# Two attention blocks in one TensorE stream: V copies placed three items ahead, output projections spread over the loop, a cast-free tail and a reordered start

## The chip, the cores and the metric

The kernel runs on one core of one Trainium2 chip; the other cores are idle. The metric is the device time of one execution in microseconds (us). Most executions of one kernel agree within 0.3%. Each experiment was timed in rounds that alternate with the kernel before on the same chip.

## The reference

Two cached attention blocks, their outputs side by side. A has 8 key/value heads, each shared by 4 of the 32 query heads; B has 32 heads of each kind. Batch 8, 64 query tokens, model width 512, 2048 cached keys, head size 128, everything in bf16.

```python
def block(x, k_cache, v_cache, wq, wo):          # A: k, v repeated 4 times along the heads
    q = (x @ wq).reshape(B, Sq, 32, 128).transpose(0, 2, 1, 3)
    p = softmax(einsum("bhqd,bhkd->bhqk", q, k) * 128 ** -0.5)
    o = einsum("bhqk,bhkd->bhqd", p, v)
    return o.transpose(0, 2, 1, 3).reshape(B, Sq, 4096) @ wo
return concatenate([block_A, block_B], axis=-1)   # 8 x 64 x 1024
```

The caches are 335 MB, each byte is used once, and the kernel transposes every K tile on the chip. On the page of the kernel before TensorE is busy 96% of the span, and the packets of the load queue take 90.7% of the span of the DMA engines.

## The kernel before

Python builds one list of operations for each engine, with hand-written semaphore waits; the order in the lists is the order on the engines. The attention work is 1024 *items*: even items are a quarter of an A half-unit (four 128-key tiles, two query heads), odd items half of a B unit (eight key tiles, one head). Sixteen items hold one A unit (one K/V head of one batch entry) and four B units. In the code `G` stands for A and `M` for B. An *evacuation* is the copy of a group's results out of PSUM, the memory that the matmuls write to.

```python
    for t in range(NI):                          # NI = 1024
        for key in chunks_at.get(t, []):
            do_chunk(key)                        # 8 key transposes (TensorE), evacuation (VectorE)
        for n in vcopies_at.get(t, []):
            do_vcopy(n)                          # V into a tile with a column of ones (VectorE)
        for use in proj_at.get(t, []):
            do_proj(use)                         # QM, QG: queries of B, A; WA, WB: output of A, B
        if t + 2 < NI:
            do_qk(t + 2)                         # scores (TensorE), exp (ScalarE)
        for gk in ot_pending.pop(t, []):
            do_ot(gk)                            # transpose of a finished output, copy (VectorE)
        do_pv(t)                                 # value product; at a group's end reciprocal, normalization
```

Where a V copy stands: five items before the first use, on VectorE, for both kinds of units. The copy also decides when the next V is requested, since the staging buffer has four slots:

```python
    def vcopy_place(n):
        f = first_item(*units[n])
        pl = f - (VLEAD_POOL if vcopy_eng(n) == "pool" else VLEAD_DVE)    # VLEAD_DVE = 5
    ...
    for it in sorted(k for k in vcopies_at if k < 0):    # before the loop: in order of slots
        for n in vcopies_at[it]:
            do_vcopy(n)
    ...
        if n >= NVT:                                     # NVT = 4, the V load of unit n
            vneeds.append(vcopy_val[n - NVT])
    reqs.sort(key=lambda r: (r[0], r[1], r[2]))          # r[0]: when the last need is produced
```

Output projections: four heads at a time, four token tiles (`tt`) of 128 rows, i.e. two batch entries each. All of them wait for the last batch entry, then come four items apart, and write the one shared PSUM bank `MISC`, which the query projections and the output transposes use too; an add on VectorE accumulates them in f32.

```python
    for s in range(NSA):
        lastL = last_item("G", s * Bn + Bn - 1)
        for tt in range(NTT):
            it = lastL + 8 + 4 * tt              # for B: lastL + 10 + 4 * tt
            if it < NI: sched(it, ("WA", s, tt))
            else: epi.setdefault(tt, []).append(("WA", s, tt))
    ...
            dvv = DV.add(lambda e, ...: e.tensor_tensor(
                outacc[:, tt, cols], region, outacc[:, tt, cols], ALU.add), ...)
            bank_reader[bank] = (dve_W, dvv)     # the bank's next writer waits for this add
```

The tail casts the sums to bf16 (two tiles on VectorE, two on ScalarE) and stores them from SyncE and ScalarE.

The softmax here doesn't subtract the row's maximum and nothing guards it: scores larger than these inputs give would overflow.

Of the kernel before, what the change touches and what calls it, by code (L numbers as in the profile page):

```python
# [4 lines left out]
ACTF = mybir.ActivationFunctionType  # L5
# [60 lines left out]
def bass_concat_heads__gqa_block_cached__mha_block_cached__near_ridge_kernel(  # L66
# [122 lines left out]
    dve_W = sem("dve_W")  # L189
    dve_F = sem("dve_F")  # L190
    pool_I = sem("pool_I")
# [77 lines left out]
    prologue_proj = []  # L269
    for h in range(HM):  # L270
        use = ("QM", h)
        if h == 0:
            prologue_proj.append(use)
        else:
            lo = 0 if h < 2 else last_item("M", (h - 2) * Bn + Bn - 1) - 1
            sched(max(lo, first_item("M", h * Bn) - 17), use)
    for hk in range(HG):
        for i in range(4):
            use = ("QG", hk, i)
            if hk == 0:  # L280
                prologue_proj.append(use)
            else:
                lo = 0 if hk < 2 else last_item("G", (hk - 2) * Bn + Bn - 1) - 1
                sched(max(lo, first_item("G", hk * Bn) - 44 + 8 * i), use)
    NSA = HG
    NSB = HM // 4
    epi = {}
    for s in range(NSA):
        lastL = last_item("G", s * Bn + Bn - 1)
        for tt in range(NTT):  # L290
            use = ("WA", s, tt)
            it = lastL + 8 + 4 * tt
            if it < NI:
                sched(it, use)
            else:
                epi.setdefault(tt, []).append(use)
    for s in range(NSB):
        lastL = last_item("M", (4 * s + 3) * Bn + Bn - 1)
        for tt in range(NTT):
            use = ("WB", s, tt)  # L300
            it = lastL + 10 + 4 * tt
            if it < NI:
                sched(it, use)
            else:
                epi.setdefault(tt, []).append(use)
# [11 lines left out]
    def V_src(kind, u):  # L317
        if kind == "G":
# [5 lines left out]
    out_v = out.rearrange("b q e -> (b q) e").rearrange("(tt p) e -> p tt e", p=P)  # L324

    PO.add(lambda e: e.memset(ident[:], 0.0), inc=pool_I)
    PO.add(lambda e: e.affine_select(out=ident[:], in_=ident[:], compare_op=ALU.not_equal,
                                     fill=1.0, base=0, pattern=[[-1, P]], channel_multiplier=1),
           needs=[(pool_I, 1)], inc=pool_I)
    for i in range(NVA):  # L330
        PO.add((lambda i: lambda e: e.memset(vaug[:, i, :, P:VW], 1.0))(i), inc=pool_I)
    PO.add(lambda e: e.memset(outacc[:], 0.0), inc=pool_I)
    PO.add(lambda e: e.memset(scr[:], 0.0), inc=pool_I)
    PO.add(lambda e: e.memset(pT[:], 0.0), inc=pool_I)
    PO.add(lambda e: e.memset(onM[:], 0.0), inc=pool_I)
    POOL_INIT_DONE = PO.count[pool_I]
    IDENT_READY = 2

    AC.add(lambda e: e.activation(scr[:, 1:2], scr[:, 0:1], ACTF.Exp), needs=[(pool_I, POOL_INIT_DONE)])
    xT_ready = {}  # L340
# [13 lines left out]
    woev_val = {}  # L354
    lastadd = {}

    for n in range(NU):
# [8 lines left out]
    def vcopy_place(n):  # L366
        f = first_item(*units[n])
        pl = f - (VLEAD_POOL if vcopy_eng(n) == "pool" else VLEAD_DVE)
        if n >= NVA:
            pl = max(pl, last_item(*units[n - NVA]) + 1)  # L370
        assert pl <= f, (n, pl, f)
        return pl
# [5 lines left out]
    def do_vcopy(n):  # L378
        needs = [(semV[n % NVT], 16 * (n // NVT + 1)), (pool_I, POOL_INIT_DONE)]
        if n >= NVA:  # L380
            occ = units[n - NVA]
            needs.append((pe_PV, pv_val[last_item(*occ)]))
        va = n % NVA
        vt = n % NVT
        if vcopy_eng(n) == "dve":
            v = DV.add(lambda e: e.tensor_copy(  # L386
                vaug[:, va, :, 0:P], vtmp[:, vt, :].rearrange("p (kt d) -> p kt d", d=P)),
                needs=needs, inc=dve_V)
            vcopy_val[n] = (dve_V, v)
        else:  # L390
            srcv = vtmp[:, vt, :].bitcast(dt.int32).rearrange("p (kt d) -> p kt d", d=P // 2)
            dstv = vaug[:, va, :, :].rearrange("p kt c -> p (kt c)").bitcast(dt.int32).rearrange(
                "p (kt c) -> p kt c", c=VW // 2)[:, :, 0:P // 2]
            v = PO.add(lambda e: e.tensor_copy(dstv, srcv), needs=needs, inc=pool_V)
            vcopy_val[n] = (pool_V, v)
# [31 lines left out]
    def do_proj(use, bank=MISC):  # L427
# [46 lines left out]
        else:  # L474
# [4 lines left out]
            ob = ob_A if prob == "A" else ob_B  # L479
            wo = wo_A if prob == "A" else wo_B  # L480
            needs.append((semWo[sl], 16 * (s // 2 + 1)))
            if prob == "A":
                lastg = ("G", s * Bn + Bn - 1, 1)
            else:
                lastg = ("M", (4 * s + 3) * Bn + Bn - 1, 0)
            needs.append((dve_C, copy_val[lastg]))

# [11 lines left out]
            if key in lastadd:  # L499
                dneeds.append((dve_W, lastadd[key]))  # L500
            dvv = DV.add(lambda e, tt=tt, cols=cols, region=region: e.tensor_tensor(  # L501
                outacc[:, tt, cols], region, outacc[:, tt, cols], ALU.add), needs=dneeds, inc=dve_W)
            lastadd[key] = dvv
# [3 lines left out]
    def do_qk(t):  # L507
# [38 lines left out]
        qk_val[t] = v  # L546
        aneeds = [(pe_S, v), (pool_I, POOL_INIT_DONE)]
        slot = t % NPT
# [10 lines left out]
    def do_pv(t):  # L559
# [31 lines left out]
        if glast:  # L591
# [12 lines left out]
            else:  # L604
# [9 lines left out]
                bank_reader[OMB] = (act_N, nv)  # L614
            norm_val[gkey] = nv

    OT_DELAY = 4

    def do_ot(gkey, bank=None):
        kind, u, pr = gkey  # L620
        bank = MISC if bank is None else bank
        needs = [(act_N, norm_val[gkey]), (pool_I, POOL_INIT_DONE)] + br(bank)
        mb = bank_bf(bank)
# [37 lines left out]
    def do_xT(prob):  # L661
# [18 lines left out]
        xT_ready[prob] = (dve_X, dv)  # L680

    do_xT("B")
    do_xT("A")

    pro_banks = [MISC, SB[0], SB[1], SB[2], OGB, OMB]
    pchunks = [k for k in chunks if chunk_slot[k] < 0]
# [36 lines left out]
    for idx, use in enumerate(epilogue_proj):  # L723
        do_proj(use, bank=epi_banks[idx % len(epi_banks)])
    act_F = sem("act_F")
    cast_val = {}
    for tt in range(NTT):
        fneeds = [(dve_W, lastadd[(tt, pr_)]) for pr_ in ("A", "B") if (tt, pr_) in lastadd]
        if tt % 2 == 0:
            v = DV.add((lambda tt: lambda e: e.tensor_copy(outbf[:, tt, :], outacc[:, tt, :]))(tt), needs=fneeds, inc=dve_F)  # L730
            cast_val[tt] = (dve_F, v)
        else:
            v = AC.add((lambda tt: lambda e: e.activation(outbf[:, tt, :], outacc[:, tt, :], ACTF.Copy))(tt),
                       needs=fneeds, inc=act_F)
            cast_val[tt] = (act_F, v)

# [28 lines left out]
    for h in range(HM):  # L765
        needs = []
        desired = first_item("M", h * Bn) - 17 - LEADW
        if h >= 2:
            needs.append((pe_W, proj_val[("QM", h - 2)]))
            needs += lead_need(desired)  # L770
        else:
            desired = -1000 + h
        src = B_wq[:, h * P:(h + 1) * P].rearrange("(ct c) d -> c ct d", c=P)
        reqs.append((SPp.need_pos(needs), desired, -1, needs,
                     (lambda sl, src: lambda e: e.dma_start(wq_M[:, sl, :, :], src))(h % 2, src), semWqM[h % 2]))
    for hk in range(HG):
        needs = []
        desired = first_item("G", hk * Bn) - 44 - LEADW
        if hk >= 2:
            needs.append((pe_W, proj_val[("QG", hk - 2, 3)]))  # L780
            needs += lead_need(desired)
        else:
            desired = -998 + hk
        src = A_wq[:, hk * 4 * P:(hk + 1) * 4 * P].rearrange("(ct c) e -> c ct e", c=P)
        reqs.append((SPp.need_pos(needs), desired, -1, needs,
                     (lambda sl, src: lambda e: e.dma_start(wq_G[:, sl, :, :], src))(hk % 2, src), semWqG[hk % 2]))
    for s in range(NSA):
        needs = []
        desired = last_item("G", s * Bn + Bn - 1) + 8 - LEADW
        if s >= 2:  # L790
# [6 lines left out]
    for s in range(NSB):  # L797
        needs = []
        desired = last_item("M", (4 * s + 3) * Bn + Bn - 1) + 10 - LEADW
        if s >= 2:  # L800
            needs.append((pe_W, proj_val[("WB", s - 2, NTT - 1)]))
        if s >= 1:
# [5 lines left out]

    SPp.add(lambda e: e.dma_start(xn_B[:, :, :], B_x.rearrange("b q c -> (b q) c").rearrange("(tt p) c -> p tt c", p=P)),
            inc=semXB, inc_by=16)  # L810
    SPp.add(lambda e: e.dma_start(xn_A[:, :, :], A_x.rearrange("b q c -> (b q) c").rearrange("(tt p) c -> p tt c", p=P)),
            inc=semXA, inc_by=16)
    for npos, desired, order, needs, fn, s_ in reqs:
        SPp.add(fn, needs=needs, inc=s_, inc_by=16)
    for tt in range(NTT):
        prog = SPp if tt % 2 == 0 else AC
        prog.add((lambda tt: lambda e: e.dma_start(out_v[:, tt, :], outbf[:, tt, :]))(tt),
                 needs=[cast_val[tt]], inc=semOut, inc_by=16)
    SPp.add(lambda e: e.wait_ge(semOut, 16 * NTT) and None, needs=[])
    AC.add(lambda e: e.wait_ge(semOut, 16 * NTT) and None, needs=[])  # L820

# [53 lines left out]
```

## Time and profile before

| | before |
|---|---|
| median of 12 runs | 1074.86 us (1073.12 to 1076.93) |
| profiled span | 1074.5 us |
| first weight load of the value product of item 0 / 16 / 1023 | 22.81 / 38.84 / 1060.24 us |
| from the last of these to the end of the span | 14.24 us |
| bytes moved | 357.13 MB, 332 GB/s over the span |

The third row divides the span into a start (to item 16), a loop and a tail. These starts are read from the timeline of weight loads. In the views, PE stands for TensorE's matmuls, PEld for its weight loads, DVE for VectorE, ACT for ScalarE, POOL for GpSimd and SP for SyncE. A line of a timeline has start and duration in us, engine, line of the kernel, operation, output<-input and shapes; in brackets, how long the engine had been idle and what released it. One more view belongs to the lines that the prediction shows: the waits of TensorE, added up by the line that waited and the line that released it (us in total, times, longest).

```profile
PE ps L631 <- DVE h L501: 7.9, 14, 0.6
PE ps L461 <- DVE h L656: 7.1, 14, 0.5
```

The first is an output transpose that waits for an output add, twice in each of seven periods; the second a query projection of A that waits for the copy of an output transpose. Both are waits for a reader of the one shared bank.

### The profile page before, as it was taken

To read this page: it belongs to the slowest core of one execution; us is meant where nothing else is said; L and a number is where in the kernel's file an instruction comes from. 1 tells how busy PE (TensorE), PEld (TensorE's weight loads), DVE (VectorE), ACT (ScalarE), POOL (GpSimd) and SP (SyncE) were. 2 spreads that over 40 slices of the span, in tenths; PEclk is the share of its full clock that TensorE was granted. 3 is DMA by queue.
4 is the path that set the end of the run, shared out by engine and by line. 5 is a ranking of instruction groups with operands and counts; after the bars stand their busy time and mean duration, and the time that the engine had idled before them with its cause. 6 is when DMAs were issued, how large, how long until landed. Compare 5 with 4: busy or idle time off the path is not lost.

```text
span 1074.5 us, 41588 instructions
## 1 busy us (share of the span) xinstructions
PE 1027.9 (96%) x18247; PEld 957.3 (89%) x18336; DVE 767.6 (71%) x1802; ACT 742.5 (69%) x1476; POOL 8.3 (1%) x17
## 2 busy tenths in 40 slices
PE   6999999999999999999999999999999999999997
PEld 4999888999889998899979999799997999979995
DVE  4777676776777767777767776677676776767775
ACT  3777766777667775677757777577775777757775
POOL 3000000000000000000000000000000000000000
PEclk9999999999999999999999999999999999999999
DMA  9999997999889998799998999899997999979991
GB/s 345 403 375 359 330 317 261 385 361 359 315 278 380 362 353 315 275 381 366 347 311 291 383 364 336 289 332 369 372 327 276 346 350 369 342 256 347 349 359 58
DMA packets 123540, 357.13 MB, mean 332 GB/s; under 512 B 27616, under 2 KB 40928, under 8 KB 123360
## 3 DMA queue, kind: packets, MB, share of 16 engines
q1 hardware_dynamic: 123072, 353.94, 90.7%
q8 instruction: 146, 2.39, 0.9%
q10 hardware_dynamic: 288, 0.52, 0.1%
q14 instruction: 34, 0.28, 0.1%
HBM read 353.37 MB, written 1.05 MB: 330 GB/s over the span
## 4 chain that ended last, share of the span: by engine, by line
PE 82%; DVE 11%; issue 2%; ACT 2%; DMA 2%; SPq 1%; DVEq 0%
PE ps L413 24%; PE ps L586 19%; PE ps L578 10%; PE ps L527 9%; PE ps L542 8%; PE ps L491 5%; DVE h L421 4%; DVE h L386 4%; PE ps L440 2%; PE ps L461 2%; DVE h L501 2%; ACT h L611 1%; PE ps L649 1%; DMA h<-in_B_v_cache_dram 1%; PE ps L631 1%
## 5 line engine op out<-in xcount | busy, mean ns | idle before, releaser
L421 DVE COPY h<-ps 128x1024 bf16<-128x1024 bf16 x640 | 440.2, 688 | 152.1 <-PE ps L413 142.6
L413 PE MATMUL ps<-h 128*128 128x128 bf16 x5120 | 390.3, 219 | 5.8 <-DMA h<-in_B_k_cache_dram 2.4
L555 ACT ACTIVATE h<-ps 128x512 bf16<-128x512 f32 x512 | 305.0, 596 | 103.3 <-PE ps L542 98.5
L550 ACT ACTIVATE h<-ps 128x512 bf16<-128x512 f32 x512 | 305.4, 597 | 91.5 <-PE ps L527 66.8
L586 PE MATMUL ps<-h 128*128 128x129 bf16 x4096 | 323.4, 220 | 6.4 <-issue 0.4
L413 PEld LDWEIGHTS ps<-h 128*128 128x128 bf16 x5120 | 314.3, 98 | 8.6 <-issue 7.1
L586 PEld LDWEIGHTS ps<-h 128*128 128x128 bf16 x4096 | 252.1, 98 | 10.6 <-issue 10.4
L386 DVE COPY h<-h 128x2048 bf16<-128x2048 bf16 x320 | 218.0, 682 | 1.2 <-DMA h<-in_B_v_cache_dram 1.2
L578 PE MATMUL ps<-h 128*128 128x129 bf16 x2048 | 203.4, 221 | 0.0
L542 PE MATMUL ps<-h 128*128 128x64 bf16 x4096 | 202.9, 193 | 0.5 <-issue 0.5
L527 PE MATMUL ps<-h 128*128 128x128 bf16 x2048 | 197.6, 219 | 0.7 <-ACT h L469 0.7
L542 PEld LDWEIGHTS ps<-h 128*128 128x128 bf16 x4096 | 169.4, 98 | 7.4 <-issue 0.8
L527 PEld LDWEIGHTS ps<-h 128*128 128x128 bf16 x2048 | 139.7, 98 | 21.7 <-ACT h L469 1.2
L578 PEld LDWEIGHTS ps<-h 128*128 128x128 bf16 x2048 | 138.6, 98 | 0.0
L611 ACT ACTIVATE h<-ps,h 64x128 bf16<-64x128 f32 x256 | 92.8, 363 | 65.3 <-DVE h L609 42.0
L600 DVE RECIPROCAL h<-ps 128x1 f32<-128x1 f32 x128 | 21.4, 167 | 74.5 <-PE ps L578 74.5
L501 DVE TENSOR_TENSOR h<-ps,h 128x512 f32<-128x512 f32 x64 | 44.1, 689 | 34.3 <-PE ps L491 34.1
L491 PE MATMUL ps<-h 128*128 128x512 bf16 x227 | 58.5, 380 | 5.0 <-ACT h L448 1.6
L649 PE MATMUL ps<-h 128*128 128x128 bf16 x256 | 56.3, 220 | 0.4 <-ACT h L611 0.4
L638 DVE COPY h<-ps 128x128 bf16<-128x128 bf16 x128 | 28.2, 220 | 33.7 <-PE ps L631 28.8
L601 ACT ACTIVATE h<-ps,h 128x128 bf16<-128x128 f32 x128 | 47.3, 369 | 0.3 <-DVE h L600 0.3
L656 DVE COPY h<-ps 128x64 bf16<-128x64 bf16 x256 | 46.4, 181 | 0.7 <-PE ps L649 0.7
(29 smaller groups left out, 266.1 us busy)
## 6 DMA issues: line engine op xcount, KB each, us to landing
h<-in_B_k_cache_dram SPq DMA_DIRECT2D x256, 512.0 KB, 6.5
h<-in_B_v_cache_dram SPq DMA_DIRECT2D x256, 512.0 KB, 6.1
h<-in_A_k_cache_dram SPq DMA_DIRECT2D x64, 512.0 KB, 5.4
h<-in_A_v_cache_dram SPq DMA_DIRECT2D x64, 512.0 KB, 7.4
h<-in_B_wq_dram SPq DMA_DIRECT2D x32, 128.0 KB, 6.8
h<-in_A_wq_dram SPq DMA_DIRECT2D x8, 512.0 KB, 7.7
h<-in_A_wo_dram SPq DMA_DIRECT2D x8, 512.0 KB, 6.2
h<-in_B_wo_dram SPq DMA_DIRECT2D x8, 512.0 KB, 7.8
```

Source lines behind the costliest of these rows:

```text
L386: v = DV.add(lambda e: e.tensor_copy(vaug[:, va, :, 0:P], vtmp[:, vt, :].rearrange("p (kt d) -> p kt d", d=P)), needs=needs, inc=dve_V)
L413: ins = e.matmul(dst[:, j * P:(j + 1) * P], lhsT=kin[:, ks, kt * P:(kt + 1) * P], rhs=ident[:, :], is_transpose=True, start=True, stop=True)
L421: dv = DV.add(lambda e, kb=kb, par=par, c=c, kTX=kTX: e.tensor_copy(kTX[:, par, 8 * c:8 * c + 8, :], bank_bf(kb)[:, 0:8 * P].rearrange("p ...
L491: ins = e.matmul(region, lhsT=ob[:, sl, hh, tt * P:(tt + 1) * P], rhs=wo[:, sl, hh, :], start=(hh == 0), stop=(hh == 3))
L527: ins = e.matmul(ps[:, sbk, j * P:(j + 1) * P], lhsT=kT_G[:, par, kt, :], rhs=rhs, start=True, stop=True)
L542: ins = e.matmul(ps[:, sbk, j * SQ:(j + 1) * SQ], lhsT=kT_M[:, par, kt, :], rhs=rhs, start=True, stop=True)
L550: av = AC.add(lambda e: e.activation(pT[:, slot, 0:512], ps[:, sbk, :], ACTF.Exp, scale=scale), needs=aneeds, inc=act_E)
L555: av = AC.add(lambda e: e.activation(dstv, srcv, ACTF.Exp, scale=scale), needs=aneeds, inc=act_E)
L578: ins = e.matmul(ps[:, OGB, 0:P + 1], lhsT=pT[:, slot, j * P:(j + 1) * P], rhs=vaug[:, va, kt, 0:P + 1], start=(kt == 0), stop=(kt == NKT ...
L586: ins = e.matmul(ps[:, OMB, 0:P + 1], lhsT=pT[:, slot, j * P:(j + 1) * P], rhs=vaug[:, va, kt, 0:P + 1], start=(kt == 0), stop=(kt == NKT ...
L611: nv = AC.add(lambda e: e.activation(onM[0:SQ, par, :], ps[0:SQ, OMB, 0:P], ACTF.Copy, scale=rsM[0:SQ, par:par + 1]), needs=[(dve_R, rv)] ...
L649: return e.matmul(mb[:, 0:P], lhsT=onM[:, par, :], rhs=ident[:, :], is_transpose=True, start=True, stop=True)
```

## The change

The intent is to remove waits from TensorE: (1) A's V copy two items later; (2) each output projection as soon as its own two batch entries are done, so that they are spread and never near another use of the shared bank; (3) a tail with three projections left instead of eight, sums written as bf16 by the last add, stores from GpSimd; (4) x and query weights of A first, finer waits for the initial fills. Core of the diff:

```diff
-        pl = f - (VLEAD_POOL if vcopy_eng(n) == "pool" else VLEAD_DVE)
+        pl = f - (3 if units[n][0] == "G" else VLEAD_DVE)
...
+    def wo_dep_unit(prob, s, tt):
+        b = BPT * tt + BPT - 1
+        return ("G", s * Bn + b, 1) if prob == "A" else ("M", (4 * s + 3) * Bn + b, 0)   # (shortened)
...
-            it = lastL + 8 + 4 * tt
+            it = last_item(gk[0], gk[1]) + 10        # WA; gk = wo_dep_unit("A", s, tt)
-            it = lastL + 10 + 4 * tt
+            it = last_item(gk[0], gk[1]) + 14        # WB
...
-            needs.append((dve_C, copy_val[lastg]))
+            needs.append((dve_C, copy_val[wo_dep_unit(prob, s, tt)]))
...
+            if s == nsess - 1:
+                dvv = DV.add(lambda e, ...: e.tensor_tensor(
+                    outbf[:, tt, cols], region, outacc[:, tt, cols], ALU.add), ...)
+                final_val[key] = dvv
...
-    (four casts of outacc to outbf, on VectorE and ScalarE; four stores, from SyncE and ScalarE)
+        PO.add((lambda tt: lambda e: e.dma_start(out_v[:, tt, :], outbf[:, tt, :]))(tt),
+               needs=[(dve_W, final_val[(tt, "A")]), (dve_W, final_val[(tt, "B")])], inc=semOut, inc_by=16)
...
-    do_xT("B")
     do_xT("A")
+    do_xT("B")
     (request order xA, wqG0, xB, wqM0 ...; exp table loaded after one small fill instead of all)
```

One side effect is not visible in the diff. The copies before the loop are emitted in order of their slots. With A's at -3 and B's still at -4, the first B copy now precedes the first A copy. The V load of the second A unit (needed at item 16) therefore enters the queue before that of the fourth B unit (needed at item 13).

## The prediction

> **What bounds the kernel now.** First the page: the span, the busy shares and the chain of work that ended last.
>
> ```profile
> span 1074.5 us, 41588 instructions
> PE 1027.9 (96%) x18247; PEld 957.3 (89%) x18336; DVE 767.6 (71%) x1802; ACT 742.5 (69%) x1476; POOL 8.3 (1%) x17
> ...
> PE 82%; DVE 11%; issue 2%; ACT 2%; DMA 2%; SPq 1%; DVEq 0%
> ```
>
> TensorE is the bound, but the weight-load row (PEld), which has a record of every load, is busy 957 of 1074 us: up to 117 us in which no new matmul started, some of it the slow tail of 512-column matmuls, the rest waits. The work is a sequence of 1024 items, alternately a quarter of an A half-unit and half of a B unit. 16 items (one A unit, four B units) are one unit of the loop; eight units are one period, after which the extras recur: 4 projections each of kinds QM and QG (queries) and WA and WB (output), 16 in all. So I cut the stretch from 540.5 to 671.7 us, one period, into its eight units, of which five are shown (the cuts are at the first weight load of each unit's first value product); columns are time, busy TensorE, loads, VectorE, ScalarE, GpSimd, clock, DMA share and GB/s.
>
> ```profile
> 540.52:560.80 20.28, 19.39 (x302) 16.42 (x303) 15.29 (x34) 11.51 (x23) 0.00 (x0) 1.00 0.91 318
> 560.80:579.16 18.36, 17.28 (x293) 15.30 (x292) 12.46 (x30) 11.57 (x23) 0.00 (x0) 1.00 0.72 230
> 579.16:594.40 15.24, 15.05 (x285) 14.54 (x284) 12.12 (x29) 11.28 (x23) 0.00 (x0) 1.00 1.01 384
> 594.40:608.77 14.37, 14.23 (x282) 14.13 (x280) 10.39 (x27) 11.26 (x23) 0.00 (x0) 1.00 0.98 373
> ...
> 657.37:671.74 14.37, 14.23 (x281) 14.13 (x279) 10.38 (x27) 11.25 (x23) 0.00 (x0) 1.00 0.94 320
> ```
>
> A unit with no projection takes 14.37 us; one QM adds 0.87 us. All eight output projections sit in the first two units, 20.28 and 18.36 us, where DMA idles; in the rest DMA is nearly full. 16 projections at 0.867 us are 13.9 us, eight bare units 115.0; the period is 131.2, so 2.35 us of it is collision. One looks like this:
>
> ```profile
> 551.55 0.69 DVE L501 TENSOR_TENSOR h<-ps,h 128x512 f32<-128x512 f32 x1 [0.17 <-PE ps L491]
> ...
> 552.30 0.10 PEld L631 LDWEIGHTS ps<-h 128*128 128x128 bf16 x1 [0.74 <-DVE h L501]
> ```
>
> All projections and all output transposes share one PSUM bank. The transpose (L631), scheduled at the same item as a WA, waits for the add (L501) that reads the bank; its loads come 0.74 us late. Even the bare unit has a wait, at items 11 to 13:
>
> ```profile
> 604.40 0.68 DVE L386 COPY h<-h 128x2048 bf16<-128x2048 bf16 x1
> ...
> 605.10 0.15 DVE L609 RECIPROCAL h<-ps 64x1 f32<-64x1 f32 x1
> ...
> 605.29 0.36 ACT L611 ACTIVATE h<-ps,h 64x128 bf16<-64x128 f32 x1 [0.66 <-DVE h L609]
> ...
> 605.76 0.48 PEld L586 LDWEIGHTS ps<-h 128*128 128x128 bf16 x8 [0.23 <-issue]
> ```
>
> The V copy of the A unit (L386) is queued on VectorE ahead of the transpose copy (at 605.00), the reciprocal (L609) and so the normalization (L611); the next value product (L586), which reuses that accumulator bank, starts late. Against the usual 0.26 us from the score loads to the value loads this took 0.56 us (605.20 to 605.76): 0.30 us lost, in most units. The page does not name it ("issue").
>
> **What the Trainium skill says.** "Perfetto Trace Analysis", Identifying the Most-Contended Engine: weight-load busy share, not matmul busy, tells the distance to the limit. The trace agrees: 89% against 96%. "TensorE: Matmul & The Clock Gate", Wait — 56ns, not 53.3ns?: warm start-to-start 55.6 ns at 128 columns and 215.7 ns at 512; here eight transposes take 447 ns to the next group, 55.9 each, and four projection matmuls 0.863 us, 215.8 each. Same page, Architectural detail: VectorE and ScalarE are strict FIFO; the L386 lines above show it. "DMA: Bandwidth & Descriptors", Specifications and Anatomy of one DMA: about 1 us to the first byte from GpSimd against 0.6 from the hardware path, some 2 us fixed cost; before, output DMAs from SP and ACT land in 2.4 to 2.6 us, and no GpSimd DMA is in this trace.
>
> **The change part by part.**
> (1) The A unit's V copy moves from 5 items before its use to 3 (item 11 to item 13). The instruction order of the changed kernel shows it right behind the B copy of item 12. VectorE then starts these two about 13.4 and 14.05 us into the unit and is free at 14.65 (spacing 0.6, from the trace), while the next reciprocal is wanted at about 14.46 and the next evacuation at 14.9. So the 0.30 us goes and nothing new waits long: bare unit 14.37 to 14.07. As a check, the load spacings sum to: ten evacuation groups x 0.447, eight A scores x 0.224, eight B scores x 0.26, eight A products x 0.232, eight B products x 0.44, six transposes 0.23 = 13.95 us. 64 units x 0.30 = 19 us at most, but those with QG at item 12 lose 0.49 there instead, counted in (2).
> (2) WA and WB are spread: WA at item 8 of even units, WB at items 5 and 13 of the units 7 and 0. Each is two or more items after the last transpose on the shared bank, or has a 0.45 us evacuation group between; the next transpose comes two items (over 2 us) later. QM at item 0 already has this distance and costs only 0.87. QG at item 12 waited 0.49 us for the transpose copy behind the V copy, twice a period; that goes with (1). So 2.35 us x 7 periods = 16 us falls to about 0.
> Loop, by sum: 63.9 units x 14.07 = 899.6; 120 projections in the loop (128 less 5 ahead, 3 behind) x 0.867 = 104.0; start waits 1.7: 1005.3 us. Before, by the same sum: 918.8 + 115 x 0.867 = 99.7 + 1.7 + 17 = 1037.4, which is the trace's 23.05 to 1060.47. Saved: 19 from the bare units and 17 from collisions, less 4.3 for five projections taken in, 32 us; less about 1 for irregular half-microseconds that a few periods show: 31.
> (3) The tail. Before:
>
> ```profile
> 1062.05 6.59 PEld L491 LDWEIGHTS ps<-h 128*128 128x128 bf16 x32 [0.42 <-DVE h L656]
> ...
> 1069.78 1.28 DVE L730 CAST h<-h 128x1024 bf16<-128x1024 f32 x2
> ```
>
> From the last value product (1060.24) to the end: 14.3 us. Eight adds, one per 0.865 us, end at 1069.86. Now three projections instead of eight follow, so the last add ends 5 x 0.865 = 4.3 us sooner, 5.3 us after that product; no cast (1.2 us), but a GpSimd DMA, estimated from the skill's page at 3 us to landing, plus 0.5 to the end: 8.9 us. Saved 5.4. The five moved projections are paid in (2).
> (4) The start. x of A and its query weights go first, the exponent table loads early, initial waits are finer. But the same bytes lie ahead of the first K, which TensorE waited for at 12.9 us; five evacuation groups and four projections still follow. Only the first score gets earlier, by about one evacuation, 0.6 us. Against it, the first V of an A unit is now requested before a B unit's V that is needed sooner, and the loads of this phase run at the limit (a V landed just before its copy at 31 us): 1.3 us later. I take +0.5 to +2.
> (5) Loads. 44 MB a period in 126.4 us are 349 GB/s. The dense six units before ran at 320 to 384 and V landed 3 us or more ahead of its copy; moving a copy later takes 2 us of that in one unit of five. I add 1.5.
> Sum: 1074.3 - 31 - 5.4 + 1.5 + 1.5 = about 1041.
>
> **Rivals.** (a) VectorE takes the place of the removed wait: with 10.4 us busy of 14.1 it has room on average, but two V copies in a row delay what follows, and a 0.1 to 0.2 us wait at items 14 to 17 would return half of (1): 1050. For it: margins are only 0.1 to 0.4 us. Against: the reciprocals after item 13 are wanted later than the copies end. (b) DMA becomes the bound: its share is 0.94 to 1.01 in six of eight units, and the rest it got in the output units goes. For it: with a full queue a 512 KB load lands every 1.26 us, with longer gaps now and then, some 370 GB/s over 46 us. Against: 349 is under that and the lead was stable. It would make 1048 to 1056. (c) The moved work only moves: if TensorE were already full, five projections in the loop would eat the tail's gain and the time would stay at 1070. Against: the load row's 117 us.
>
> **Range and chances.** 1041; everything as summed without (5) gives 1037, slightly better 1034; half of (1) lost or DMA short gives 1051. 2% faster is 1052.8. Chances: faster 0.9, within 2% 0.09, slower 0.01.
>
> **What would show it.** Bare pace: a unit with one projection at 14.9 us, the period at 126 to 127; no transpose waiting for an output add; the value product at item 13 starting 0.26 us after the scores' loads; three projections and no cast at the end, the span's last 9 us after the last value product; start no better. I am wrong if units stay near 14.4, if value copies wait for V loads in mid-run, or if the GpSimd stores take over 5 us.

## The result, and the profile after

The changed kernel takes 1038.5 us, median of 8 runs (1037.1 to 1039.6); the ratio to the kernel before is 0.9661, 95% interval 0.9651 to 0.967. Ratios here are the mean time of one kernel's fast runs over the mean of the other's of the same rounds, so not quite the ratio of the medians quoted. That is 36.4 us, 3.4% faster.

The page after: span, busy shares, chain of work that ended last.

```profile
span 1037.0 us, 41555 instructions
PE 1013.4 (98%) x18215; PEld 955.5 (92%) x18336; DVE 771.2 (74%) x1800; ACT 746.7 (72%) x1474; POOL 10.6 (1%) x21
...
PE 96%; DMA 2%; issue 1%; SPq 0%; DVE 0%; POOL 0%; ACT 0%
```

The weight-load row, which holds the same 18336 loads, has the same busy time; only the gaps between loads are gone, from 117 to 82 us. In the chain VectorE fell from 11% to 0%: TensorE no longer waits for a VectorE operation in the loop.

Three units of one period (656.68 to 783.03 us), in the columns of the prediction:

```profile
656.68:674.20 17.52, 17.31 (x294) 15.63 (x296) 14.12 (x32) 11.55 (x23) 0.00 (x0) 1.00 0.98 335
674.20:688.28 14.08, 14.08 (x282) 14.08 (x280) 10.49 (x26) 11.47 (x23) 0.00 (x0) 1.00 0.94 329
688.28:704.07 15.79, 15.68 (x288) 14.85 (x288) 12.75 (x30) 11.36 (x23) 0.00 (x0) 1.00 1.03 384
```

In the bare unit (second line) weight loads are busy for all of 14.08 us: there is nothing left to remove but work. Four projections cost 17.52 - 14.08 = 3.44 us, two cost 1.71, that is 0.86 each, with no collision. The period is 126.35 us instead of 131.2.

The place of the old wait, the value product at item 13, in the timeline (start, duration, engine, line):

```profile
714.45 0.16 DVE L618 RECIPROCAL h<-ps 64x1 f32<-64x1 f32 x1
714.64 0.36 ACT L620 ACTIVATE h<-ps,h 64x128 bf16<-64x128 f32 x1
...
715.10 0.33 PEld L551 LDWEIGHTS ps<-h 128*128 128x128 bf16 x8
715.36 0.48 PEld L595 LDWEIGHTS ps<-h 128*128 128x128 bf16 x8
715.50 1.28 DVE L393 COPY h<-h 128x2048 bf16<-128x2048 bf16 x2
```

The reciprocal and the normalization now come before the V copies (L393, two in a row). The value loads (L595) start 0.26 us after the scores' loads (L551), where it was 0.56.

The longest entries of TensorE's waits after:

```profile
PE ps L682 <- DMA h<-in_A_x_dram: 4.5, 1, 4.5
PE ps L420 <- DVE h L428: 2.8, 1, 2.8
PE ps L420 <- DMA h<-in_B_k_cache_dram: 1.7, 1, 1.7
```

All are single waits of the start. In the loop no transpose waits for an output add and no projection for a copy (in the tail one projection still waits 0.3 us for a copy). But 2.8 us behind an evacuation (L428) is new. It is at 31 to 34 us. Three lines of the timeline: VectorE and the weight loads after, then the same copy before.

```profile
32.91 0.69 DVE L393 COPY h<-h 128x2048 bf16<-128x2048 bf16 x1 [5.20 <-DMA h<-in_B_v_cache_dram]
...
34.25 0.77 PEld L420 LDWEIGHTS ps<-h 128*128 128x128 bf16 x8 [2.99 <-DVE h L428]
```

```profile
31.23 0.69 DVE L386 COPY h<-h 128x2048 bf16<-128x2048 bf16 x1 [1.22 <-DMA h<-in_B_v_cache_dram]
```

The B unit's V landed about one load later, and the copy that waits for it stood at the head of VectorE's queue for 5.20 us. The evacuations behind it could not run, so TensorE stood still for 2.99 us. What came then is in the windows of the stretch (the number before the last two is the granted clock):

```profile
32.00:34.00 2.00, 0.00 (x0) 0.00 (x0) 1.09 (x2) 0.00 (x0) 0.00 (x0) 1.00 1.07 360
34.00:36.00 2.00, 1.74 (x21) 1.75 (x22) 1.60 (x5) 0.24 (x1) 0.00 (x0) 0.52 1.05 406
36.00:37.00 1.00, 1.00 (x12) 1.00 (x10) 0.28 (x3) 0.43 (x2) 0.00 (x0) 0.50 1.01 401
```

After the stall TensorE ran at half clock from about 34.1 to 37.5 us: a group of eight transposes took 0.77 and 0.90 us of loading instead of 0.49. In the kernel before, the clock stays at 1.00 here.

The tail after:

```profile
1030.08 2.27 PEld L495 LDWEIGHTS ps<-h 128*128 128x128 bf16 x12 [0.43 <-DVE h L665]
...
1032.89 0.69 DVE L506 TENSOR_TENSOR h<-ps,h 128x512 bf16<-128x512 f32 x1 [0.17 <-PE ps L495]
...
1033.87 0.54 POOL L735 DMA_DIRECT2D out_dram<-h  x1 [1.19 <-DVE h L506]
```

Twelve loads (three projections) instead of 32, a last add that writes bf16, no cast, and a GpSimd store from whose issue to the end 3.1 us pass.

| stretch of the profile | before | after | difference |
|---|---|---|---|
| start, to item 16 | 38.84 | 41.72 | +2.9 |
| loop, item 16 to item 1023 | 1021.4 | 986.55 | -34.9 |
| tail | 14.24 | 8.71 | -5.5 |
| span | 1074.5 | 1037.0 | -37.5 |

The loop of the kernel before has a few irregular half-microseconds: two experiments below with an unchanged loop have 1019.4 and 1018.8. Against those the loop gained 32.5 us.

### The profile page after: what moved, and what is told of

Its sections match the earlier page's. It is cut to its first block, busy times and chain, and to the rows that moved or that the text cites.

```text
span 1037.0 us, 41555 instructions
## 1 busy us (share of the span) xinstructions
PE 1013.4 (98%) x18215; PEld 955.5 (92%) x18336; DVE 771.2 (74%) x1800; ACT 746.7 (72%) x1474; POOL 10.6 (1%) x21
## 4 chain that ended last, share of the span: by engine, by line
PE 96%; DMA 2%; issue 1%; SPq 0%; DVE 0%; POOL 0%; ACT 0%
PE ps L420 27%; PE ps L595 23%; PE ps L587 11%; PE ps L551 11%; PE ps L536 11%; PE ps L495 5%; PE ps L447 2%; PE ps L468 2%; PE ps L658 1%; DMA h<-in_B_v_cache_dram 1%; DMA h<-in_A_k_cache_dram 1%; PE ps L640 1%; DVE h L393 0%; SPq L791 0%; SPq L758 0%
## 5 line engine op out<-in xcount | busy, mean ns | idle before, releaser
L428 DVE COPY h<-ps 128x1024 bf16<-128x1024 bf16 x640 | 441.7, 690 | 164.3 <-PE ps L420 152.4
L564 ACT ACTIVATE h<-ps 128x512 bf16<-128x512 f32 x512 | 305.6, 597 | 96.2 <-PE ps L551 92.3
L559 ACT ACTIVATE h<-ps 128x512 bf16<-128x512 f32 x512 | 306.6, 599 | 93.8 <-PE ps L536 65.1
L595 PE MATMUL ps<-h 128*128 128x129 bf16 x4096 | 323.8, 221 | 0.3 <-issue 0.3
L595 PEld LDWEIGHTS ps<-h 128*128 128x128 bf16 x4096 | 252.4, 98 | 0.5 <-issue 0.5
L393 DVE COPY h<-h 128x2048 bf16<-128x2048 bf16 x320 | 213.3, 683 | 5.2 <-DMA h<-in_B_v_cache_dram 5.2
L551 PE MATMUL ps<-h 128*128 128x64 bf16 x4096 | 203.0, 193 | 0.9 <-ACT h L455 0.6
L551 PEld LDWEIGHTS ps<-h 128*128 128x128 bf16 x4096 | 169.7, 98 | 8.2 <-issue 1.1
L495 PE MATMUL ps<-h 128*128 128x512 bf16 x195 | 52.3, 379 | 3.5 <-DVE h L665 0.3
L476 ACT ACTIVATE h<-ps 128x512 bf16<-128x512 f32 x32 | 19.1, 597 | 35.1 <-PE ps L468 35.1
```

Source lines behind the costliest of these rows:

```text
L393: v = DV.add(lambda e: e.tensor_copy(vaug[:, va, :, 0:P], vtmp[:, vt, :].rearrange("p (kt d) -> p kt d", d=P)), needs=needs, inc=dve_V)
L428: dv = DV.add(lambda e, kb=kb, par=par, c=c, kTX=kTX: e.tensor_copy(kTX[:, par, 8 * c:8 * c + 8, :], bank_bf(kb)[:, 0:8 * P].rearrange("p ...
L495: ins = e.matmul(region, lhsT=ob[:, sl, hh, tt * P:(tt + 1) * P], rhs=wo[:, sl, hh, :], start=(hh == 0), stop=(hh == 3))
L551: ins = e.matmul(ps[:, sbk, j * SQ:(j + 1) * SQ], lhsT=kT_M[:, par, kt, :], rhs=rhs, start=True, stop=True)
L559: av = AC.add(lambda e: e.activation(pT[:, slot, 0:512], ps[:, sbk, :], ACTF.Exp, scale=scale), needs=aneeds, inc=act_E)
L564: av = AC.add(lambda e: e.activation(dstv, srcv, ACTF.Exp, scale=scale), needs=aneeds, inc=act_E)
```

## The experiments

The theory: (1) and (2) take out 0.30 us per unit and the bank collisions, and the moved projections pay for themselves; the start's swap of two V loads costs what the tail partly brings. Rivals: only one of the two loop parts works and the other is carried along; loads are so near their limit that they hold back the rest; the distance of three items matters, not what the copy stands behind. Four kernels do one part each on the kernel before, the others alter the changed kernel. All gave correct results. The line numbers of a kernel shift by a few with its edits.

**The V copy alone** (the kernel before with one line changed).

```diff
-        pl = f - (VLEAD_POOL if vcopy_eng(n) == "pool" else VLEAD_DVE)
+        pl = f - (3 if units[n][0] == "G" else VLEAD_DVE)
```

> The kernel before with one line changed: the A units' V copy placed 3 items before its use instead of 5. Theory (the copy stands in VectorE's queue ahead of the reciprocal that the value product at item 13 waits for): a bare unit goes from 14.37 to 14.07 us, 19 us in all; the projections at item 12 lose their 0.49 us wait too, 2.7 us more; the start loses about 2 us because a V load is requested out of order. About 1055 us against 1075. Rival (VectorE is too full and the wait only moves to the next reciprocal): bare unit stays above 14.3, time 1070 or more.

Measured: 1061.52 us, ratio 0.988 (0.9866 to 0.9893), some 13 us less rather than about 20. Part of what is missing is the start: item 16 comes at 41.54 us, 2.7 later than before, because this one line already swaps the two V loads. The rest is in the units that hold the output projections (windows of this kernel):

```profile
533.74:554.47 20.73, 19.60 (x306) 16.41 (x304) 15.43 (x34) 11.57 (x23) 0.00 (x0) 1.00 0.88 330
554.47:572.52 18.05, 17.17 (x293) 15.23 (x291) 12.56 (x29) 11.78 (x23) 0.00 (x0) 1.00 0.70 225
```

The first grew from 20.28 to 20.73, while the other seven units of a period became 0.30 to 0.46 us shorter. Its timeline at items 13 and 14 shows why:

```profile
548.51 1.29 DVE L386 COPY h<-h 128x2048 bf16<-128x2048 bf16 x2
...
549.71 0.69 DVE L501 TENSOR_TENSOR h<-ps,h 128x512 f32<-128x512 f32 x1
...
550.45 0.55 PEld L491 LDWEIGHTS ps<-h 128*128 128x128 bf16 x4 [0.74 <-DVE h L501]
```

The V copies that moved to item 13 now precede the add of a WB, and the next output projection waits for that add. In this one unit of eight the removed wait came back as a wait for the shared bank. A period lost 1.98 us in all, 131.22 to 129.24 (sums of the median units).

**The spread alone** (the kernel before with `wo_dep_unit`, its two item formulas, its needs, and the earlier weight loads).

```diff
-            it = lastL + 8 + 4 * tt
+            it = last_item(gk[0], gk[1]) + 10
-            it = lastL + 10 + 4 * tt
+            it = last_item(gk[0], gk[1]) + 14
```

> The kernel before with the output projections spread over the period, each as soon as its own tokens are done (and their weights requested accordingly), nothing else. Theory (collisions on the one shared PSUM bank): 2.35 us a period over 7 periods, less the 0.38 us a period of the projections at item 12, which stays: 13.8 us; the five projections taken from the tail into the loop cost there what the tail gains. About 1061 us against 1075. Rival (the spread projections collide with other transposes instead): 1070 or more.

Measured: 1054.12 us, ratio 0.9812 (0.9797 to 0.9827), some 20 us less rather than 14. A unit with four projections and a bare one:

```profile
535.78:553.29 17.51, 17.51 (x298) 15.62 (x295) 13.97 (x32) 11.43 (x23) 0.00 (x0) 1.00 0.94 337
553.29:567.66 14.37, 14.23 (x282) 14.14 (x280) 10.42 (x26) 11.31 (x23) 0.00 (x0) 1.00 0.94 332
```

The bare unit still has its 0.30 us wait, 14.37. But the unit with a WB at item 13 is at 17.51, just as in the changed kernel: the projection stands where the wait was and fills it. So part of the item-13 wait goes with either part alone. The loop is 1002.8 us here and 1003.6 with the copy alone, against 1018.8 to 1019.4: -16.3 and -15.5 from the middle of those, together -31.8, and both in one kernel give -32.5. So each loop part is worth about half, and the two add up to within 0.7 us: with the spread in place the copy still brings 16.2 us (1002.8 to 986.55), against 15.5 alone.

**The tail alone** (the kernel before with the last add into the bf16 tile and the GpSimd stores; eight projections remain).

```diff
+            if s == nsess - 1: ... e.tensor_tensor(outbf[:, tt, cols], region, outacc[:, tt, cols], ALU.add)
-    (casts, stores from SyncE and ScalarE)
+    (stores from GpSimd)
```

> The kernel before with the last add writing bf16 straight to the output tile and GpSimd storing, all else as before (eight projections still at the end). Theory: the two casts, 1.2 us, go, the store path costs no more: 1073.7 against 1074.9. Rival (the GpSimd store path costs more than the casts did): 1075 or more.

Measured: 1073.1 us, ratio 0.9986 (0.998 to 0.9993). The tail is 13.02 instead of 14.24 us. These 1.2 us are for casts and stores together: the GpSimd stores, as an experiment below shows in the changed kernel, have a tail 0.9 us longer than hardware stores, so that the casts alone come to some 2.1 (an estimate from the two). From 13.02 to the 8.71 of the changed kernel are 4.3 us, the five projections of 0.865 that moved; the spread alone, which keeps the casts, likewise has a tail of 9.94, 4.3 less than 14.24.

**The start alone** (the kernel before with A first, the new request order, the finer initial waits).

```diff
-    do_xT("B")
     do_xT("A")
+    do_xT("B")
     ... and the request order and initial waits of the change
```

> The kernel before with the start alone changed: x and query weights of A first, order of the initial memsets and finer initial waits. Theory (the start is bound by loads, whose bytes do not change; what cost 2.9 us in the changed kernel at the end of the first unit is the order of two V loads, which comes from moving the V copy, not from this part): the first value product about 2 us earlier, the second unit no earlier or up to 1 us earlier: 1074 to 1075. Rival (the start's reordering itself costs): about 1077.

Measured: 1075.77 us, ratio 1.0007 (1.0001 to 1.0014). Item 16 comes at 39.51 us against 38.84. The start part gains nothing, and taken alone it costs under a microsecond.

**The order of the two V loads** (the changed kernel; copies before the loop in order of units again).

```diff
-    for it in sorted(k for k in vcopies_at if k < 0):
-        for n in vcopies_at[it]:
-            do_vcopy(n)
+    for n in sorted(n for k in vcopies_at if k < 0 for n in vcopies_at[k]):
+        do_vcopy(n)
```

> The changed kernel with the V copies ahead of the first item issued in the units' order again (A's first, then B's), so that the V load needed first is requested first; nothing else. Theory (the swapped request makes a V land one load, 1.28 us, later, and the stall in VectorE's queue holds TensorE long enough to slow its clock): the second unit starts 2.7 us earlier, the rest is unchanged: 1035.8 against 1038.5, ratio to before 0.9637. Rival (the start is bound by its bytes, not by their order): 1038.5.

Measured: 1036.17 us, ratio 0.9642 (0.9628 to 0.9657), about 2 us better than the changed kernel, though the two intervals overlap by a little. The copy that stalled:

```profile
31.35 0.69 DVE L393 COPY h<-h 128x2048 bf16<-128x2048 bf16 x1 [3.72 <-DMA h<-in_B_v_cache_dram]
```

Its V landed in time to start it at 31.35 us instead of 32.91. The clock is 1.00 throughout the stretch from 30 to 40 us, and item 16 comes at 38.71, 3.0 earlier. So the 2.9 us that the start lost are those of the swap. The trace of the kernel with hardware stores (below), whose start is that of the changed kernel, separates what they consist of. There the same stall came, but the clock stayed full:

```profile
32.62 0.69 DVE L393 COPY h<-h 128x2048 bf16<-128x2048 bf16 x1 [5.06 <-DMA h<-in_B_v_cache_dram]
...
33.96 0.45 PEld L420 LDWEIGHTS ps<-h 128*128 128x128 bf16 x8 [2.97 <-DVE h L428]
```

The eight loads took 0.45 us, not 0.77, and item 16 came at 39.98. That is 1.27 us after the kernel with the order mended, as much as the copy is later (32.62 less 31.35). In the changed kernel the copy is 0.29 us later still, but item 16 is 1.74 later: the remaining 1.45 us are the half clock. So the swap always delays the landing, but it does not always bring the half clock: of the four traces with a stall of 2.97 to 3.01 us here, three have it (the changed kernel, the copy alone, 4.7% more bytes). The changed kernel's own eight runs differ in the same way: two have a mean granted clock of 1.0 (1037.1 and 1037.56 us), the other six one of 0.996 to 0.998 (1037.64 to 1039.6 us).

**Four items instead of three** (the changed kernel).

```diff
-        pl = f - (3 if units[n][0] == "G" else VLEAD_DVE)
+        pl = f - (4 if units[n][0] == "G" else VLEAD_DVE)
```

> The changed kernel with the A units' V copy 4 items before its use (item 12) instead of 3. Theory (what counts is only that the copy stands behind item 11's reciprocal in VectorE's queue): bare unit stays at 14.07; and the copies ahead of the first item fall into the units' order again, so the start's 2.7 us come back: 1035.8, as with the request order alone. Rival (the distance itself counts, and one item less gives part of the wait back): bare unit 14.15 to 14.3, 1040 or more.

Measured: 1037.09 us, ratio 0.9651 (0.9636 to 0.9665). Four items also put the first copies back in order (item 16 at 38.87). By time it cannot be told from the changed kernel or from the one with the repaired order. The loop is 2.2 us longer than in the changed kernel, but the median length of each of the eight units of a period is the same to 0.01 us. The difference is seven irregular pauses between items 128 and 1008, 3.3 us in all, where the changed kernel has three of 1.2 us. They fall inside a group of matmuls, as in this line of the timeline, where one load of eight came before the pause and seven after it:

```profile
1006.09 0.45 PEld L595 LDWEIGHTS ps<-h 128*128 128x128 bf16 x7 [0.67 <-issue]
```

No wait of the kernel stands there. What counts for the regular pace is that the copy is behind the reciprocal of item 11, not whether it is at item 12 or 13.

**Stores from the hardware queues** (the changed kernel; SyncE and ScalarE issue them in turn).

```diff
-        PO.add((lambda tt: lambda e: e.dma_start(out_v[:, tt, :], outbf[:, tt, :]))(tt),
+        prog = SPp if tt % 2 else AC
+        prog.add((lambda tt: lambda e: e.dma_start(out_v[:, tt, :], outbf[:, tt, :]))(tt),
```

> The changed kernel with its four stores issued by SP and ScalarE instead of GpSimd. Theory (issue 0.54 us and some 2.6 us to the end from GpSimd, 0.44 and some 2.5 from the others): within 0.5 us of 1038.5. Rival (GpSimd's path is a microsecond slower[...]): about 1037.5.

Last add and last store:

```profile
1030.48 0.69 DVE L506 TENSOR_TENSOR h<-ps,h 128x512 bf16<-128x512 f32 x1 [0.17 <-PE ps L495]
1031.20 0.34 SPq L822 DMA_DIRECT2D out_dram<-h  x1
```

The store is issued 0.72 us after the add's start instead of 0.98, and the end follows 2.5 us later (span 1033.7) instead of 3.1. The tail is 7.81 us instead of 8.71, more than the half microsecond that I had allowed and nearer to the rival's microsecond. In time it does not show: 1038.07 us, ratio 0.9657 (0.9641 to 0.9673) against 0.9661. (The profiled run, 1035.46 us, is the fastest of the four; the others, at a lower mean clock, took 1037.53 to 1039.48.)

**More bytes to load** (the changed kernel; for each A unit, half or all of its K once more into a tile that nobody reads). The rival that loads hold the kernel back says that 4.7% or 9.5% more bytes must cost about as much time.

```diff
+        if kind == "G":
+            eneeds = needs + ([(semE, 16 * u)] if u else [])
+            reqs.append((SPp.need_pos(needs), desired, 2 * n, eneeds,
+                         (lambda src: lambda e: e.dma_start(spare[:, :], src))(K_src(kind, u)[:, 0:1024]), semE))
```

(`0:2048` and a spare tile of twice the size in the second kernel.)

> The changed kernel with one more load of 256 KB per A unit into a spare tile that nothing reads: 2.1 MB more a period, 366 GB/s in place of 349. Theory (loads are near but not at their limit): up to 3 us slower, 1041 at most, with V landing later. Rival (the changed kernel is already bound by its loads): slower by the bytes, 4.7%: about 1085.

> The changed kernel with one more load of 512 KB per A unit that nothing reads: 382 GB/s asked for in place of 349. Theory (with a full queue the loads of the kernel before ran at some 370 GB/s over 46 us): now the loads bound it, 48.4 MB a period at 372 GB/s are 130 us in place of 126.4: 1060 to 1070. Rival (the loads have more room than that): 1045 or less.

Measured: 1041.2 us, ratio 0.9682 (0.9666 to 0.9699) with 4.7% more; 1045.03 us, ratio 0.9725 (0.9711 to 0.974) with 9.5% more. So 2.3 and 6.9 us, 0.2% and 0.7%; the interval of the first overlaps that of the changed kernel (0.9651 to 0.967). Of the first, 1.3 us are the start (item 16 at 43.02). I had expected the second at 1060 to 1070 and was wrong. Its page, and its wait for V loads:

```profile
DMA packets 132500, 390.69 MB, mean 375 GB/s; under 512 B 28640, under 2 KB 41952, under 8 KB 132320
...
DVE h L395 <- DMA h<-in_B_v_cache_dram: 10.3, 8, 7.0
```

The loads ran at 375 GB/s over the whole span, where the changed kernel needs 344. Of the 10.3 us, 7.0 are the stall of the start. After 45 us five V copies wait for their loads, 1.4 us in all; in the changed kernel none does, and in every other kernel at most one, of up to 0.6 us. The 370 GB/s that I had read from a dense stretch of the kernel before was the rate that the kernel asked for, not the rate that the loads can reach; a DMA share of 1.0 did not mean that no more could be moved.

**The old start** (the changed kernel with the order of the V loads repaired and the start of the kernel before).

```diff
-    do_xT("A")
     do_xT("B")
+    do_xT("A")
     ... request order, initial fills and their waits as in the kernel before
```

> The changed kernel with the start of the kernel before (x and query weights of B first, the old order of memsets and waits), and with the V copies ahead of the first item in the units' order; copy place, spread projections and tail as changed. Theory (the start part alone cost 0.7 us when put into the kernel before, and what it wins ahead of the first value product is lost to the loads): 0.7 us faster than the changed kernel with the request order mended, ratio to before 0.9635. Rival (in the faster kernel the early start counts): ratio 0.965 or more.

Measured: 1035.94 us, ratio 0.9643 (0.963 to 0.9657); with the new start it was 0.9642. Part (4) of the change is worth nothing that these runs can show (the interval is 1.5 us either way). (One of the runs of the kernel before took 2852.43 us; it is not a fast run and is in no ratio.)

**Weights out of the first loads** (four items, and 1.7 MB of weights that are used later are requested later).

```diff
-            desired = -500                          # wq of B, head 1: last of the initial requests
+            desired = 1000
-            desired = -499                          # wq of A, head group 1: after its item
+            needs += lead_need(desired)
-        if s >= 1:
-            needs += lead_need(desired)             # both wo: also the first ones wait
+        needs += lead_need(desired)
```

> The changed kernel with the V copy 4 items ahead (which also mends the request order) and with the weights that are not needed in the first 16 items (the second query weights of both, the first output weights of both, 1.7 MB) requested later, by the progress of the items. Theory (the first unit waits for loads queued behind those): the second unit starts about 4 us earlier, at 34 to 35.5 us; ratio to before 0.961 to 0.962, about 1033. Rival (the bytes must be loaded anyway and the wait comes back within the first period): ratio 0.964 or more.

Measured: 1035.15 us, ratio 0.9639 (0.9623 to 0.9654). Item 16 comes at 35.47 us, 3.4 earlier than with four items alone. But item 128 comes at 147.05 against 147.7: almost all of it is given back in the first period, and the ratio is above the 0.961 to 0.962 that I had expected. It is not shown that the deferred bytes take it back, as the rival has it. TensorE waits for no load there; 2.5 of the 2.7 us given back are two pauses inside groups of matmuls, 0.9 and 1.6 us (units of 16.72 and 17.38 us where 15.8 is usual). The next kernel, with the same loads, has only the first of them, and its item 128 comes at 145.65.

**Both ends** (the same, hardware stores, and one of the three last projections ahead of the last output transposes, in another bank).

```diff
+    first_epi = epilogue_proj.pop(0)
+    do_proj(first_epi, bank=SB[1])
+    held = DV.ops.pop()                             # its add: after the transposes' copies
     for it in sorted(ot_pending.keys()):
         for gk in ot_pending[it]:
             do_ot(gk)
+    DV.ops.append(held)
```

> The kernel with late weights and, at the end, the stores issued by SP and ScalarE and one of the last three projections moved ahead of the last two output transposes, with its add behind their copies. Theory: the end after the last value product falls from 8.7 to about 7 us; 1.7 us less than with late weights alone: ratio 0.9595, about 1031. Rival (the wait for the last normalization bounds the end anyway): no change.

Measured: 1033.44 us, ratio 0.962 (0.9606 to 0.9634), the best of all, 41 us under the kernel before and 0.4% under the changed one. The expected ratio was 0.9595. The tail is 7.59 us where about 7 was expected: against 7.81 with hardware stores alone, the projection moved ahead brings 0.2.

| kernel | median us | item 16 | loop | tail |
|---|---|---|---|---|
| before | 1074.86 | 38.84 | 1021.4 | 14.24 |
| changed | 1038.5 | 41.72 | 986.6 | 8.71 |
| copy alone | 1061.52 | 41.54 | 1003.6 | 14.26 |
| spread alone | 1054.12 | 38.98 | 1002.8 | 9.94 |
| tail alone | 1073.1 | 38.88 | 1019.4 | 13.02 |
| start alone | 1075.77 | 39.51 | 1018.8 | 14.27 |
| order of V loads | 1036.17 | 38.71 | 986.0 | 8.72 |
| four items | 1037.09 | 38.87 | 988.8 | 8.71 |
| hardware stores | 1038.07 | 39.98 | 985.9 | 7.81 |
| 4.7% more bytes | 1041.2 | 43.02 | 988.0 | 8.69 |
| 9.5% more bytes | 1045.03 | 42.59 | 990.5 | 8.72 |
| old start | 1035.94 | 38.75 | 986.7 | 8.72 |
| late weights | 1035.15 | 35.47 | 991.4 | 8.72 |
| both ends | 1033.44 | 35.66 | 990.5 | 7.59 |

## Why the prediction was right

The time, 1038.5 for 1041 us, and the range held. Step by step:

- **The bound and the bare unit: right.** The unit went to 14.08 us (14.07 predicted), with weight loads busy for all of it. The wait behind the V copy, which the page before names only as "issue", was real, and the reader of the timeline finds it where the prediction put it.
- **Collisions and moved projections: right together, mis-sized apart.** The period is 126.35 us, eight bare units and sixteen projections with nothing over; "126 to 127" was said. The loop gained 32.5 to 34.9 us for the 31 predicted; the larger figure holds the irregular half-microseconds that the prediction took off. The split was off: of the loop's gain it gave 19 us to the copy and 11.7 (16 less 4.3) to the spread; alone they brought some 15.5 and 16.3. The copy's term counted all eight units of a period, but with the copy alone the unit with crowded output projections grew by 0.44 us, because it hands the wait on to the shared bank; and a WB at item 13 fills the same wait, so that there the 0.30 us belong to whichever part comes first. (A slip in the sums: 918.8 + 99.7 + 1.7 + 17 is 1037.2, not 1037.4.)
- **The tail: right.** 8.71 us for 8.9, and its terms too: 4.3 for five projections, 1.2 for casts and stores together. The estimate of 3.5 us from a GpSimd store to the end measured 3.4 from the last add to the end of the span, with some luck: the last store is issued 0.29 us after the add and lands 2.3 us later, not 3, but 0.8 us follow, not 0.5.
- **The start: the right cause, too small.** +2.9 us for +1.5. The landing of the B unit's V was 1.6 us later, for 1.3. What the prediction left out is that the copy waiting for it holds up the evacuations behind it on VectorE, so that TensorE stood still and in this trace then ran at half clock for some 3.4 us, which cost 1.45 us. The 0.6 us counted as a gain is not to be seen: item 0 comes at 20.48 us after. Five traces have the old start. In the two whose clock stayed full from 12 to 17 us, item 0 comes at 20.02 and 20.14; in the three with a stretch of half clock there (before, spread alone, old start) at 21.59 to 22.81. None of this reaches item 16, which comes at 38.75 to 38.98 in those three and at 38.88 with the tail alone, whose clock stayed full.
- **Loads: the term of +1.5 us was wrong.** It did not occur. With 9.5% more bytes the bare unit is still at 14.07 us, and the whole costs 6.9 us. The rival (b), a load limit near 370 GB/s, fell with the 375 GB/s measured.
- **Rival (a)**, VectorE in the place of the removed wait, did not occur in the changed kernel, and three or four items made no difference. It did occur with the copy alone: there the add behind the copies was the new wait. **Rival (c)**, moved work that only moves, is refuted by the spread alone: 4.3 us came off the tail and the loop got shorter as well.

Start 1.4 us more than predicted, loop 3.9 less, loads 1.5 less, tail 0.1 less: together 4.1, from 1041 to the profiled span of 1037.0 (that start and loads cancel is luck); the timed median lies 1.5 above that span. One sign was put wrongly: no unit holds a single projection, they hold none, two or four. What stays open is where the pauses inside groups of matmuls come from, which are most of what profiles of one loop differ by; no run here changed them on purpose. The packed traces hold a hint: the page lists a queue `q8 instruction` with 146 packets of 16 KB, some 7 us apart, and all ten pauses counted above for the changed kernel and for four items end 2.2 to 2.6 us after such a packet starts. That TensorE waits there for its own instructions is an inference from these times and not tested.

## What to carry to other kernels

A copy of 0.69 us on an engine that is busy only 71% of the span can cost the busiest engine 0.30 us an iteration if it stands ahead of a short operation in the same queue; look at where the next weight load starts, not at the page's sums of waits, and move the copy behind. Two changes that remove waits on the same stretch should be measured one at a time and together: here each alone was worth about half, and one of them, alone, handed its wait on in one unit of eight. And when a request order is derived from a slot number, compare the order of the first few requests too: a swap of two loads that the diff doesn't show cost 3 us in the profile, a twelfth of the gain.

## What the Trainium skill lacked or had wrong

- "DMA: Bandwidth & Descriptors", Where 436 GB/s comes from: for transfers between HBM and SBUF it says that the HBM side, about 358 GB/s, binds. This one core, with the others idle, moved 375 GB/s as a mean over 1041.8 us with 9.5% extra loads (372 GB/s of it from and to HBM), and over 400 in several fortieths of that span (406 the highest), so that figure is no limit for a core that runs alone. A table further down the page, under iDMA fabric, agrees better: it has 408.7 for the load stream of one core alone.
- "TensorE: Matmul & The Clock Gate", Back-to-back issue gap: it gives a sustained spacing of about 131 ns for matmuls of 512 columns and about 81 ns for 128 columns in a stream of weight loads and matmuls. Here four projection matmuls of 512 columns, each with its own weight load, take 0.865 us, 216 ns each, and transposes of 128 columns follow each other at 55.9 ns; the figures that the page calls those of an isolated matmul are the ones that hold in this stream.
- "TensorE: Matmul & The Clock Gate", Why this matters for your kernels: it warns of idle gaps above some 3 us between matmuls. The gaps here lie at that edge: between matmul records 2.81 us in the changed kernel, with half clock after it, and 2.79 us with hardware stores, without. What no page has is the way into such a gap: a copy waits for a late load at the head of VectorE's queue (5.20 us), and TensorE stalls behind the evacuations (2.99 us between weight loads). Where the clock fell it cost about as much again (1.45 us) as the late landing itself (1.6 us).
- No page has a number for the pauses inside a group of matmuls, without any wait of the program, that recur at the same items in different kernels: 0.2 to 0.9 us each, three in the changed kernel and seven with four items between items 128 and 1008, all ending 2.2 to 2.6 us after a packet of the queue `q8 instruction` starts.
